# RWKV attention and an FFN in one launch: the bonus sums of chunk 1 by GpSimd and VectorE in place of TensorE, u's transfer in two parts, and a new order

## The chip, the cores and the metric

The kernel runs on one core of a Trainium2 chip. The core has TensorE (PE: matmuls; its weight loads are shown apart as PEld), VectorE (DVE), ScalarE (ACT), GpSimd (POOL) and SyncE (SP), which here only issues transfers; 16 DMA engines move data between HBM and the on-chip memory. TensorE writes to PSUM, which has eight banks of 512 float32 columns in 128 partitions. The metric is the time of one execution on the device in microseconds (us): 522.6, the median of three (520.49, 522.60, 523.03). The trace shown here is of a fourth execution, of 521.4 us.

## The reference

Inputs: r, k, v, w of shape 4 x 8 x 768 x 48 (batch, head, time, dimension), u of 8 x 48, and two FFN weights of 384 x 2048 and 2048 x 384, all float32. For each batch and head a 48 x 48 state runs through time; then each of the 3072 tokens goes through the FFN.

```
for t in range(S):
    cur = einsum('bhd,bhe->bhde', u * k[t], v[t])
    y[t] = einsum('bhd,bhde->bhe', r[t], state + cur)
    state = w[t][..., None] * state + einsum('bhd,bhe->bhde', k[t], v[t])
x = y.transpose(0, 2, 1, 3).reshape(B * S, H * D)
out = square(maximum(x @ w_in, 0)) @ w_out
```

The term of `cur` in y is, for each token and head, a scalar (the sum over d of r u k) times v. These scalars, 8 for each of 128 tokens of a unit, are the bonus sums.

## The kernel before

**The work.** Time is cut into 6 chunks of 128; a unit is one chunk of one batch, so there are 24. For a unit, running products of w (scans, L535) turn the recurrence into matmuls in the chunk and a state that is carried on. For chunks 0 and 1, TensorE turns w, k and r into the layout with the dimension on the partitions (`turn`, L516); for later chunks VectorE and transfers do it. Then `scores` (L750 for chunk 0, L671 for the rest), `mix` and the state's `outer` run on TensorE. A chunk's four units end in x, which is split into two float32r parts; the FFN goes over 16 blocks of 128 hidden units (f): 9 matmuls into one of two hp buffers (L860), relu and square on ScalarE and VectorE (L865 to L872), then 3 matmuls for each batch into the four ob banks (L878). Chunks 0 and 1 start their FFN in halves of two batches, so "hp at 0" to "hp at 11" are half blocks of 256 columns.

**The weights** come in eight groups (ri, ro for w_in and w_out as loaded; wi, wo as split). Each half of a group goes through ScalarE (L428), three VectorE steps on the bits (L432, L436, L441), ScalarE (L448) and a GpSimd subtraction (L449). All of it falls into the first 125 us.

**The bonus sums.** In chunks 0 and 1 (`c < 2`), VectorE multiplies the turned r and k into a buffer m (L550), TensorE multiplies that with u in 4 matmuls of 4 columns (`betas`, L575), for chunk 1 into an hp buffer, and ScalarE copies the result to beta in two copies (`place_betas`, L581). In chunks 2 to 5, GpSimd multiplies r by k and by -u as they were loaded, with time on the partitions (L584, L586), VectorE sums over the dimension (L589) and swaps halves between partitions in three small copies (`halves`, L592 to L594). From beta, ScalarE makes the diagonal blocks (L630, L745) on which `mix` builds.

**u** is loaded once, on ScalarE's queue, as one row repeated in all 128 partitions (un, L389); TensorE turns it for chunks 0 and 1 (L384), and GpSimd changes its sign for the later ones (L392).

**The order.** Each operation is a step of a plan with its engine, reads and writes; a table ORDER gives the order of all steps, found by a search beforehand, PLACES the buffer that each slot takes, and FILLS the places where a step on TensorE is preceded by filler: transposes of the identity into a free part of a bank (`fill`, L347), which nobody reads. An engine runs its steps strictly in that order. A step may not start before the steps whose data it reads or overwrites have ended. Some tiles lie on top of each other: chunk 1's x (`x1`) and the r, k, w of chunk 1's batches 2 and 3, and the raw weights of the last two groups and tiles of the first chunks.

Of the kernel before, what the change touches and what calls it, by code (L numbers as in the profile page):

```python
# [96 lines left out]
class Names:  # L97
# [132 lines left out]
def kernel(  # L230
# [11 lines left out]
    nc = tc.nc  # L242
# [34 lines left out]
    PC = J - D  # L277
# [48 lines left out]
    P = Plan()  # L326
# [129 lines left out]
    def attention(c, b, rank):  # L456
# [109 lines left out]

        rk = lambda: vals(1)
        beta = Slot("beta")
        if c < 2:
            bp = Slot("hp") if c else ps[0]  # L570
            bt = lambda: tl(bp) if c == 0 else bp.tile

# [446 lines left out]
```

## Time and profile before

| | |
|---|---|
| median of three executions | 522.6 us |
| the profiled execution | 521.4 us |
| its span in the trace | 519.7 us |
| TensorE busy | 506.6 us, 97% |
| VectorE busy | 358.3 us, 69% |
| ScalarE busy | 319.1 us, 61% |
| GpSimd busy | 87.8 us, 17% |
| HBM read, written | 31.65 MB, 4.72 MB |

The span is what the trace shows from the first to the last instruction; the execution's own time is 1.7 us longer. Busy times are the sum of an engine's instructions; matmuls are pipelined, so a busy TensorE need not be at its peak, and filler counts as busy. "idle before" names the wait of an engine and, behind an arrow, what ended it. The trace shows one matmul of float32 as two.

### The profile page before, as it was taken

How to read it: one execution, taken by the hardware profiler on the slowest of the kernel's cores; microseconds unless marked ns; L12 is line 12 of the kernel's file. 1: busy time of each engine (PE TensorE's matmuls, PEld its weight loads, DVE VectorE, ACT ScalarE, POOL GpSimd, SP SyncE). 2: the span in 40 equal slices, each digit the busy share in tenths (PEclk: the TensorE clock that was granted, in tenths of full speed). 3: DMA queues.
4: the chain of work that ended last, by engine and by line, in shares of the span. 5: the costliest groups of instructions: out<-in, count | busy, mean ns of one | idle time of the engine just before them, and what ended most of it. 6: DMA issues, size and time to landing. Idle time of an engine off the chain costs nothing.

```text
span 519.7 us, 13752 instructions
## 1 busy us (share of the span) xinstructions
PE 506.6 (97%) x5452; PEld 458.5 (88%) x5452; DVE 358.3 (69%) x787; ACT 319.1 (61%) x878; POOL 87.8 (17%) x133
## 2 busy tenths in 40 slices
PE   8999999999999999999998999999999999999996
PEld 7888898888999998899987989889988888998895
DVE  6999789898687988768778658678476354333332
ACT  4999898996766867666573656564543363433232
POOL 3025233344021040212203001303000000000000
PEclk9999999999999999999999999999999999999999
DMA  7999977363847765575772480661181000100001
GB/s 152 225 165 247 246 151 205 88 92 63 148 71 100 147 97 95 106 125 73 117 129 37 84 137 15 112 122 36 32 133 32 3 19 6 59 16 0 1 2 65
DMA packets 188310, 48.74 MB, mean 94 GB/s; under 512 B 178000, under 2 KB 183120, under 8 KB 188240
## 3 DMA queue, kind: packets, MB, share of 16 engines
q1 hardware_dynamic: 187520, 46.82, 47.6%
q8 instruction: 45, 0.74, 0.6%
q10 hardware_dynamic: 720, 0.98, 0.5%
q14 instruction: 25, 0.20, 0.1%
HBM read 31.65 MB, written 4.72 MB: 70 GB/s over the span
## 4 chain that ended last, share of the span: by engine, by line
PE 78%; SPq 5%; issue 5%; DVE 4%; ACT 4%; DMA 2%; POOL 1%; POOLq 0%; ACTq 0%; DVEq 0%
PE ob L878 35%; PE hp L860 34%; PE ob L668 2%; SPq L504 2%; PE ob L687 2%; DMA ri<-in_moe_w_in_dram 2%; PE a L677 2%; SPq L415 1%; PE a L650 1%; PE hp L635 1%; SPq L471 1%; POOL wi L449 1%; DVE pt L535 1%; ACT t L865 1%; DVE m L550 1%
## 5 line engine op out<-in xcount | busy, mean ns | idle before, releaser
L878 PE MATMUL ob<-wo,g 128*128 128x384 f32 x1152 | 227.0, 340 | 0.1
L860 PE MATMUL hp<-x,wi 128*128 128x512 f32 (+1 forms) x1062 | 221.8, 355 | 3.2 <-DVE g L872 2.5
L878 PEld LDWEIGHTS ob<-wo,g 128*128 128x128 f32 x1152 | 199.4, 188 | 8.1 <-DVE g L872 0.9
L860 PEld LDWEIGHTS hp<-x,wi 128*128 128x128 f32 x1062 | 174.1, 188 | 29.7 <-DVE g L872 3.7
L869 DVE SCALAR_TENSOR_TENSOR hp<-hp,t 128x512 f32<-128x512 f32 (+1 forms) x96 | 58.2, 606 | 74.5 <-ACT t L865 74.2
L865 ACT ACTIVATE t<-hp 128x512 f32<-128x512 f32 (+1 forms) x118 | 61.0, 517 | 72.2 <-PE hp L860 47.7
L872 DVE TENSOR_TENSOR g<-hp,g 128x512 fp32r<-128x512 f32 (+1 forms) x118 | 69.1, 587 | 35.5 <-ACT g L871 35.0
L871 ACT CAST g<-hp 128x512 fp32r<-128x512 f32 (+1 forms) x118 | 59.6, 506 | 49.5 <-DVE hp L869 48.6
L630 ACT ACTIVATE m<-diag,beta 128x64 f32<-128x64 f32 x160 | 40.4, 338 | 3.4 <-DVE beta L593 3.3
L658 POOL MEMSET S<- 1x1 f32 x20 | 2.2, 110 | 237.4 <-PE ob L668 237.4
L614 DVE SCALAR_TENSOR_TENSOR x<-ob,x 112x128 fp32r<-112x128 f32 x80 | 21.2, 284 | 19.3 <-ACT x L611 16.5
L822 ACT COPY ob<-zero 112x128 f32<-112x128 f32 x80 | 20.7, 270 | 17.3 <-PE ob L878 10.1
L611 ACT ACTIVATE x<-ob 112x128 fp32r<-112x128 f32 x80 | 19.1, 275 | 17.3 <-PE ob L687 12.1
L535 DVE TENSOR_TENSOR_SCAN pt<-pt,zero 112x128 f32<-112x128 f32 x64 | 27.2, 456 | 2.4 <-DMA x<-x 1.1
L449 POOL TENSOR_TENSOR wi<-q,wi 128x768 fp32r<-128x768 f32 x8 | 17.1, 2135 | 55.1 <-ACT wi L448 44.0
L584 POOL TENSOR_TENSOR st<-st 128x384 f32<-128x384 f32 x16 | 16.7, 1043 | 33.0 <-DVE st L480 32.5
L480 DVE STREAM_TRANSPOSE st<-st 128x1152 f32<-128x1152 f32 x16 | 21.6, 1363 | 0.0
L542 ACT ACTIVATE m<-pt 112x512 f32<-112x512 f32 x24 | 15.1, 631 | 9.2 <-DVE pt L535 8.2
L449 POOL TENSOR_TENSOR wo<-q,wo 128x768 fp32r<-128x768 f32 x8 | 15.9, 1983 | 18.1 <-ACT wo L448 14.8
L558 DVE TENSOR_TENSOR pt<-pt,m 112x512 f32<-112x512 f32 x24 | 16.9, 706 | 2.4 <-ACT Ec L557 1.3
L559 DVE SCALAR_TENSOR_TENSOR m<-pt,m 112x512 f32<-112x512 f32 x24 | 18.0, 748 | 0.3
L709 DVE COPY_PREDICATED m<-caus,a 128x256 f32<-128x256 uint8 x40 | 17.3, 439 | 0.9 <-PE a L650 0.9
(125 smaller groups left out, 540.0 us busy)
## 6 DMA issues: line engine op xcount, KB each, us to landing
pt<-st SPq DMA_DIRECT2D x96, 96.0 KB, 2.9
ro<-in_moe_w_out_dram SPq DMA_DIRECT2D x8, 768.0 KB, 6.1
v<-in_v_dram SPq DMA_DIRECT2D x96, 48.0 KB, 2.8
out_dram<-q SPq DMA_DIRECT2D x20, 192.0 KB, 2.1
ri<-in_moe_w_in_dram SPq DMA_DIRECT2D x32, 96.0 KB, 4.9
ri<-in_moe_w_in_dram SPq DMA_DIRECT2D x8, 384.0 KB, 6.1
st<-in_r_dram SPq DMA_DIRECT2D x8, 384.0 KB, 5.3
st<-in_w_dram SPq DMA_DIRECT2D x8, 384.0 KB, 4.9
```

The source lines that it names most:

```text
L449: P.add("pool", 1.9, rank(8 * k + 5), lambda q=q, tt=tt: G.tensor_tensor(out=tt[:, 1], in0=q.tile, in1=tt[:, 0].bitcast(F32), op=ALU.subtr ...
L480: V.transpose(out=zt[:, i].rearrange("a t p q i -> a t (p q) i"), in_=sv[:, :, i].rearrange("s t p q x -> s t (p q) x"))
L535: lambda p=p: V.tensor_tensor_scan(out=pt[:, 0, p], data0=src(0)[:, p], data1=zero.broadcast_to([HP, C]), initial=1.0, op0=ALU.mult, op1=A ...
L614: made.append(P.add("dve", c2, rank(nm + "l"), lambda y=y, hi=hi, lo=lo: V.scalar_tensor_tensor(out=lo(), in0=y(), scalar=-1.0, in1=hi().b ...
L630: A.activation(M.tile[:, o:o + Q], diag2, AF.Copy, scale=beta.tile[:, i:i + 1])
L822: P.add("act", 0.16, rank("zero"), lambda p=p: A.copy(out=obs[p][0:HP, DM:], in_=zero[0:HP].broadcast_to([HP, C])), w=[("YO", p)], after=t ...
L860: T.matmul(hp.tile[:, 0:n], wi[f][:, wl, kt], xT[:, kt, xl, xs], start=(m == 0), stop=(m == 3 * KT - 1))
L865: P.add("act", 0.49 if full else 0.28, rank("g1"), lambda: A.activation(t(), h(), AF.Relu), r=[hp], w=[(g, 1)])
L869: P.add("dve", 0.605 if full else 0.337, rank("g2"), lambda: V.scalar_tensor_tensor(out=h(), in0=h(), scalar=0.0, in1=t(), op0=ALU.max, op ...
L871: P.add("act", 0.48 if full else 0.26, rank("g3"), lambda: A.copy(out=hi(), in_=h()), r=[hp], w=[(g, 0)])
L872: P.add("dve", 0.605 if full else 0.335, rank("g4"), lambda: V.tensor_tensor(out=lo(), in0=h(), in1=hi().bitcast(F32), op=ALU.subtract), r ...
L878: T.matmul(obs[b][:, 0:DM], g.tile[0][:, gl, o:o + C], wo[f][:, wl], start=(f == 0 and m == 0), stop=(f == NF - 1 and m == 2))
```

## The change

1. In chunk 1 the bonus sums are made as in chunks 2 to 5: GpSimd multiplies twice, VectorE sums and swaps. The product on VectorE, the matmuls on TensorE and the copies on ScalarE stay for chunk 0 alone.
2. u's first transfer, on ScalarE's queue, fills one partition, and all of un is set to zero by VectorE beforehand (a wider memset). TensorE's turn of u, which takes the first row, stays. A second transfer of all 128 rows is issued on SP later, and GpSimd's change of sign comes behind it.
3. ORDER, PLACES and FILLS are new throughout. FILLS had 52 transposes at 12 places and has 57 at 13.

```
 ORDER = (
-    4, 14, 17, 19, 6, 16, 0, 5, 20, 1, 18, 26, 15, 11, 7, 23, 24, 25, 55, 58, 309, 21, 22, 27, 28, 8, 2, 13, 30, 9, 57, 31, 312, 59, 33, 56, 64, 10, 29, 61,
...
 FILLS = {
-    16: (2, 'ob', 1), 55: (6, 'ob', 3), 30: (3, 'ob', 1), 57: (4, 'ob', 1), 71: (2, 'ob', 0), 48: (5, 'ob', 1), 82: (3, 'ob', 3), 89: (5, 'ob', 1),
-    145: (3, 'ob', 0), 144: (7, 'ob', 0), 127: (8, 'side', 0), 168: (4, 'side', 0),
+    17: (3, 'ob', 1), 16: (3, 'ob', 2), 56: (3, 'ob', 1), 57: (4, 'ob', 1), 42: (3, 'ob', 1), 49: (2, 'ob', 1), 83: (3, 'ob', 3), 90: (18, 'ob', 1),
+    160: (4, 'ob', 0), 469: (2, 'ob', 0), 128: (2, 'side', 0), 130: (3, 'side', 0), 192: (7, 'side', 0),
 }
...
-    V.memset(front_un[:, 0:PC], 0.0)
+    V.memset(front_un, 0.0)
...
-        P.add("actq", 0.5, "un", lambda: nc.scalar.dma_start(out=un, in_=u.rearrange("h d -> (h d)").partition_broadcast(128)), w=["un"], runs=128, issue=0.36)
+        P.add("actq", 0.1, "u0", lambda: nc.scalar.dma_start(out=un[0:1], in_=u.rearrange("h d -> (h d)").partition_broadcast(1)), w=["un"], runs=1, issue=0.36)
         P.add("pe", 0.8, "ut", turn, r=["un"], w=[up])
         P.add("act", 0.25, "ut", spread, r=[up], w=["ut"])
+        P.add("sp", 0.5, "un", lambda: nc.sync.dma_start(out=un, in_=u.rearrange("h d -> (h d)").partition_broadcast(128)), w=["un"], runs=128, issue=0.6)
...
-        if c < 2:
+        summed = c == 0
+        if summed:
             P.add("dve", 0.62, rank("rk"), lambda: V.tensor_tensor(out=Ms[0].tile[0:HP].rearrange("a (g q t) -> a q g t", q=2, g=4), in0=turned(pt[:, 1]), in1=turned(src(2)), op=ALU.mult),
...
-        if c < 2:
+        if summed:
             bp = Slot("hp") if c else ps[0]
```

Three places of the order matter below. The first is TensorE behind the state matmuls of chunk 0's last batch, where the first of chunk 1's four groups with ut (L575) stands in the kernel before:

```order
L790 MATMUL a_153<-v_94,m_165 48x48
L860 MATMUL hp_152<-x_142,wi_57 128x256 x9
L575 MATMUL hp_151<-ut,m_167 128x4 x4
L878 MATMUL ob_147<-wo_67,g_97 128x384 x3
L878 MATMUL ob_148<-wo_67,g_99 128x384 x3
L860 MATMUL hp_151<-x_142,wi_57 128x256 x9
```

In the changed kernel, behind the same state matmuls (its lines are 2 higher):

```order
L792 MATMUL a_153<-v_94,m_166 48x48
L880 MATMUL ob_147<-wo_63,g_95 128x384 x3
L862 MATMUL hp_152<-x_142,wi_57 128x256 x9
L880 MATMUL ob_147<-wo_67,g_97 128x384 x3
L862 MATMUL hp_151<-x_142,wi_57 128x256 x9
L880 MATMUL ob_148<-wo_67,g_97 128x384 x3
```

No group with ut stands there or later, and the hp buffers pass from one block of the FFN to the next. The second place is GpSimd from the second half of weights 1 on (wo_63), before:

```order
L449 TENSOR_TENSOR wo_63<-q_155,wo_63 128x768
L449 TENSOR_TENSOR wo_67<-q_156,wo_67 128x768
L449 TENSOR_TENSOR wi_69<-q_155,wi_69 128x768
L449 TENSOR_TENSOR wo_75<-q_156,wo_75 128x768
L449 TENSOR_TENSOR wi_73<-q_155,wi_73 128x768
```

And in the changed kernel (wi_69 is the first half of weights 3):

```order
L450 TENSOR_TENSOR wo_63<-q_155,wo_63 128x768
L393 TENSOR_SCALAR un<-un 128x384
L450 TENSOR_TENSOR wo_67<-q_156,wo_67 128x768
L586 TENSOR_TENSOR st_143<-st_143 128x384
L588 TENSOR_TENSOR st_143<-st_143,un 128x384
L586 TENSOR_TENSOR st_143<-st_143 128x384
L588 TENSOR_TENSOR st_143<-st_143,un 128x384
L450 TENSOR_TENSOR wi_69<-q_155,wi_69 128x768
```

u's change of sign, which stood at the head of GpSimd's queue, and the products of chunk 1's batches 1 and 0 now stand between the subtractions; those of batches 2 and 3 stand in the same way before the second half of weights 6. The third place is VectorE's three steps on the first half of weights 0 (q_155 from ri_56), before:

```order
L432 TENSOR_SCALAR q_155<-q_155 128x768
L812 TENSOR_TENSOR S_137<-a_154,Ec_169 112x96
L436 SCALAR_TENSOR_TENSOR q_155<-ri_56,q_155 128x768
L441 SCALAR_TENSOR_TENSOR q_155<-ri_56,q_155 128x768
L550 TENSOR_TENSOR m_166<-pt_136,ob_149 112x2x4x64
L552 TENSOR_TENSOR pt_136<-pt_136 112x4x127
```

And in the changed kernel:

```order
L433 TENSOR_SCALAR q_155<-q_155 128x768
L814 TENSOR_TENSOR S_137<-a_153,Ec_169 112x96
L437 SCALAR_TENSOR_TENSOR q_155<-ri_56,q_155 128x768
L552 TENSOR_TENSOR m_166<-pt_136,ob_149 112x2x4x64
L554 TENSOR_TENSOR pt_136<-pt_136 112x4x127
L442 SCALAR_TENSOR_TENSOR q_155<-ri_56,q_155 128x768
```

Two products of chunk 0's batch 2 have moved ahead of the third step. SP's first transfers are the same in kind, in another order, and u's 128 rows are its 46th.

## Rows read from the trace of the kernel before

**Rows 1.** The page, part 1: busy us, share of the span, instructions.

```profile
PE 506.6 (97%) x5452; PEld 458.5 (88%) x5452; DVE 358.3 (69%) x787; ACT 319.1 (61%) x878; POOL 87.8 (17%) x133
```

**Rows 2.** Stretches: from:to, its us, busy us (instructions) of each engine, PEclk, DMA, GB/s.

```profile
5.30:28.00 22.70, 21.76 (x326) 19.20 (x327) 19.45 (x44) 17.79 (x56) 3.00 (x2) 1.00 0.93 202
...
28.00:58.00 30.00, 27.50 (x352) 24.66 (x351) 26.66 (x47) 27.33 (x72) 10.92 (x5) 1.00 0.95 218
...
58.00:112.00 54.00, 52.97 (x491) 47.76 (x490) 48.11 (x78) 50.62 (x119) 17.08 (x11) 1.00 0.74 160
...
120.00:510.00 390.00, 387.52 (x4103) 352.08 (x4094) 252.88 (x581) 212.36 (x603) 49.23 (x91) 1.00 0.41 70
```

**Rows 3.** Timeline of TensorE: start us, us, instruction, count. Two of four L575 groups.

```profile
58.74 0.95 PE L575 MATMUL hp<-ut,m 112*128 112x4 f32 x8
...
59.55 1.31 PE L878 MATMUL ob<-wo,g 128*128 128x384 f32 x6
...
107.80 1.05 PE L575 MATMUL hp<-ut,m 112*128 112x4 f32 x8
...
108.72 1.30 PE L878 MATMUL ob<-wo,g 128*128 128x384 f32 x6
```

**Rows 4.** Groups by line: shapes, count | busy us, mean ns | idle before.

```profile
L550 DVE TENSOR_TENSOR m<-pt 112x512 f32<-112x512 f32 x4 | 4.4, 1102 | 0.0
...
L584 POOL TENSOR_TENSOR st<-st 128x384 f32<-128x384 f32 x16 | 16.7, 1043 | 33.0 <-DVE st L480 32.5 <-issue 0.3 <-DVE hp L869 0.3
...
L586 POOL TENSOR_TENSOR st<-st,un 128x384 f32<-128x384 f32 x16 | 16.5, 1033 | 0.9
...
L589 DVE TENSOR_REDUCE beta<-st 128x8 f32<-128x384 f32 x16 | 8.7, 542 | 0.0
...
L581 ACT COPY beta<-hp 64x8 f32<-64x8 f32 x8 | 1.3, 157 | 0.1
...
L593 DVE TENSOR_TENSOR beta<-beta 64x4 f32<-64x4 f32 x16 | 2.8, 173 | 0.6
...
L351 PE MATMUL ob<-ident 128*128 128x128 f32 x52 | 8.1, 283 | 0.0
```

**Rows 5.** Timeline of GpSimd, two of its subtractions on weights.

```profile
49.75 2.36 POOL L449 TENSOR_TENSOR wo<-q,wo 128x768 fp32r<-128x768 f32 x1 [2.11 <-ACT wo L448]
...
64.00 2.22 POOL L449 TENSOR_TENSOR wi<-q,wi 128x768 fp32r<-128x768 f32 x1 [8.30 <-DMA ri<-in_moe_w_in_dram]
```

**Rows 6.** The page, parts 2 and 6: GB/s by slice; u's transfer.

```profile
GB/s 152 225 165 247 246 151 205 88 92 63 148 71 100 147 97 95 106 125 73 117 129 37 84 137 15 112 122 36 32 133 32 3 19 6 59 16 0 1 2 65
...
un<-in_u_dram ACTq DMA_DIRECT2D x1, 192.0 KB, 3.9
```

**Rows 7.** Timeline of TensorE, the head.

```profile
5.58 1.07 PE L518 MATMUL ob<-ident,st 128*112 128x128 f32 x4 [0.31 <-DMA st<-in_w_dram]
...
6.87 0.83 PE L518 MATMUL ob<-ident,st 128*112 128x128 f32 x4
```

**Rows 8.** Timelines of ScalarE and VectorE, the head.

```profile
8.20 0.68 ACT L545 ACTIVATE pt<-ob,one_sided 112x512 f32<-112x512 f32 x1
...
8.93 0.69 DVE L550 TENSOR_TENSOR m<-pt,ob 112x512 f32<-112x512 f32 x1 [0.87 <-ACT pt L545]
```

**Rows 9.** Timeline of TensorE, ahead of the first FFN matmul.

```profile
26.15 0.74 PE L351 MATMUL ob<-ident 128*128 128x128 f32 x5
...
26.83 0.68 PE L790 MATMUL a<-v,m 64*64 64x48 f32 x32
...
27.44 2.42 PE L860 MATMUL hp<-x,wi 128*128 128x256 f32 x18
```

**Rows 10.** Timelines of VectorE and TensorE near 52 us.

```profile
50.46 2.47 DVE L441 SCALAR_TENSOR_TENSOR q<-ro,q 128x768 uint32<-128x768 uint32 x1
...
53.31 0.65 PE L518 MATMUL hp<-ident,st 128*112 128x128 f32 x4 [0.87 <-DVE g L872]
```

**Rows 11.** One line of VectorE: count, ns min/median/max, first and last start.

```profile
L559 DVE SCALAR_TENSOR_TENSOR m<-pt,m x24: 676/684/1514, 11.3 to 425.6; 112x512 f32<-112x512 f32 x24
```

201 rows, old and new, of tables (ORDER, PLACES) are left out of this document.

## The prediction

> **What bounds the kernel now.** I read the busy times first: TensorE 97% of the span, VectorE 69%, ScalarE 61%, GpSimd 17% [rows 1]. Shares over the whole span mix stages, so next came the stretches. From 120 to 510 us TensorE is busy 387.5 of 390 us with the others far from full: there every matmul removed is time saved. The three stretches before, 5.3 to 112 us, hold the attention of chunks 0 and 1, the splitting of the weights, and all that this change touches; TensorE stands idle there for 106.70 - 102.23 = 4.5 us, and in the last of them (58 to 112 us) only 1.03 of 54 us, while ScalarE is idle for 3.4 and VectorE for 5.9 [rows 2]. So TensorE sets the pace, but with two neighbours close behind: that is the doubt in this case. The granted clock is 1.00 throughout, the level of 2.4 GHz, and no term hangs on it.
>
> **The change part by part.**
>
> *The products for the bonus sums leave TensorE.* Chunk 1 has four groups of L575, one for each batch: 4 matmuls, which the trace counts as 8. From the start of a group to the start of the next work: 0.81 us at 58.74, 0.92 at 107.80 [rows 3], and 0.81 for each of the two between. That is 3 x 0.81 + 0.92 = 3.35 us off TensorE, all within the stretch of 58 to 112 us where it is idle 2% of the time. ScalarE loses 8 copies of 0.157 = 1.26 us [rows 4]. Four tenancies of the two hp buffers, which the first FFN matmuls also use, go as well.
>
> *What comes in.* GpSimd gets eight products, four of 1.043 and four of 1.033 us: 8.3 us [rows 4]. They lie in two blocks of 4.15 us. The first comes, with the sign change of u, before the rest of weights 3; there GpSimd waits 8.30 us for a transfer today [rows 5], and the block with the sign change (1.17 us) takes 5.3: hidden. The second lies before the rest of w_out of group 6, whose first user (f = 12) comes several matmul groups later. VectorE loses four products (4.4 us as measured; 2.74 at 0.684, the median of L559 with the same shape) [rows 4, 11] and gets four sums of 0.542 and twelve swaps of 0.173: 4.2 us [rows 4]. So VectorE gains between -0.2 and +1.5 us. I take +1.4, because the long one among the four is a stall and not work. SP issues one transfer more, u's other rows; it stands as SP's 46th, behind chunk 1's r, and holds the queue behind it for one issue of 0.6 us; the loads of weights 3 and 4 wait behind it.
>
> *u's transfer.* Of 192 KB at the head one row stays. At the 152 GB/s of the first 13 us those 192 KB were 1.3 us of traffic, shared with w, r and k [rows 6]. TensorE's first transpose waits 0.31 us for w beyond its filler [rows 7], and that is all this end can give back. The next link is r's copy on ScalarE at 8.20, behind which VectorE starts at 8.93 after 0.87 us of idle time [rows 8]. It now stands ahead of the small copy of Ec, and r was turned at 7.70 [rows 7]: about 0.45 us. Together up to 0.76 us earlier. Against it stands the third shift step on weights 0: two products of batch 2, of 0.69 us each [rows 8], are now ahead of it, and the first FFN matmul hangs on that chain; today it starts at 27.44 [rows 9]. That may cost up to 1.4 us less what the head gained. I take -0.2 with the ends -0.8 and +1.0. The larger memset on VectorE lies ahead of its first scan, where it waits for TensorE, and u's single row has until r is turned.
>
> *Filler.* The table of fills has 57 in place of 52. Five cost 0.68 us at 26.15 [rows 9], so +0.7 us if nothing waits under them, 0 if it does. Eighteen of them now stand ahead of the outer products of batch 1: 2.4 us, just before the first FFN matmul. I take +0.7.
>
> *The order.* Every step of the first 120 us may stand elsewhere; from the last 250 steps of VectorE and ScalarE on nothing moved. The 4.5 us of idle time and the 52 x 0.136 = 7.1 us of filler [rows 2, 4] are what a new order can win; the 3.35 us are what it can fail to use. No row tells which; I take 0, with these ends.
>
> Sum: -3.35 + 0.7 - 0.2 = -2.85 us. The profiled execution took 521.4 us (span 519.7 and 1.7 around it), the three timed ones 522.6 in the middle, 520.49 to 523.03; the mean of all four is 521.9. So 521.9 - 2.85 = 519.0 us.
>
> **A rule that speaks against it.** A VectorE step on weights that started at 50.46 us took 2.47; a GpSimd subtraction ran from 49.75 to 52.11, so that the step ended 0.8 us after it, and TensorE then waited 0.87 us for the VectorE step behind [rows 5, 10]. The Trainium skill ("SBUF — State Buffer", Who interferes with whom) says that a VectorE instruction with two SBUF inputs and a GpSimd instruction that reads SBUF exclude each other for a whole instruction. By that rule the trace agrees here, and each new product can stop VectorE for its whole length, 8.3 us in all.
>
> **The rivals.**
>
> *ScalarE and VectorE take the place.* In 58 to 112 us a stretch shorter by 3.35 would be 50.65 us, with 49.6 us of TensorE, 50.62 - 1.26 = 49.4 of ScalarE and 48.11 + 1.4 = 49.5 of VectorE: all near 98%, which three engines that wait for each other have not reached in any stretch [rows 2]. If the most loaded stays where ScalarE is now (93.7%), the stretch gives back only 1.26/0.937 = 1.35 us; with the filler and the head that is -0.85: 521.0 us. For it: those rows. Against: the steps may slip past 112 us, where both have room.
>
> *The new order also closes old gaps.* Half of the 4.5 us of idle time beside the sum: 521.9 - 2.85 - 2.25 = 516.8 us. For it: several of the gaps are single waits for one VectorE step, as at 52.4 us [rows 10]. Against: more filler is laid in, not less.
>
> *GpSimd stops VectorE (slower).* Place: the two blocks. If all 8 products block in full, VectorE needs 49.5 + 8.3 = 57.8 us for the 54 us stretch: +3.8, with filler and head +4.3, 526.2 us. It eats into the gain from 50.65 - 49.5 = 1.1 us of blocking on, turns it into a loss from 54 - 0.5 - 49.5 = 4.0 us, and makes the kernel slower by over 0.5% from about 7.3 us on: nearly all eight. Against it: 32 such products run in chunks 2 to 5 today, and among 24 VectorE products of the same shape the longest of one line is 1.514 us against 0.684, so a hit there cost 0.8 us [rows 11].
>
> *The removed products were hidden.* Not likely: at 58.74 and 107.80 FFN matmuls follow at once [rows 3]. Then +0.5 and 522.4 us.
>
> **How the numbers follow.** My forecast 0.45 (its own range 517.4 to 520.0, by filler, head and 0.8 us of order); two neighbours full 0.26; gaps closed 0.14; hidden 0.08; VectorE stopped 0.07. 0.5% of 522.6 is 2.6 us, about what a measurement of this kernel can tell from no change: faster means under 520.0. The forecast gives 0.42 of its 0.45, the closed gaps 0.13, the full neighbours 0.03: 0.58. Slower, over 525.2, gets half of the last and a little for waits I have not seen: 0.06. The rest, 0.36, is within. The range, 515.8 to 522.4, leaves out the blocking case and the far ends of the order.
>
> **What would show it.** In the profile after: no matmul with ut as an input later than 40 us; TensorE's busy time down by 2.5 to 3.5 us; eight more GpSimd products near 1.04 us, the first four between 52 and 64 us with the rest of weights 3 not later than 67; VectorE products at 0.69 us with one or two over 1.2; the first copy on ScalarE before 8.0 us; the first FFN matmul between 26.5 and 28.5 us. TensorE's idle time in 58 to 112 us says which case it is: near 1 us for the forecast, over 2.5 us for the full neighbours. I am wrong if GpSimd waits for u's late rows, if VectorE has several steps over 2 us under the new products, or if chunk 1's first outputs on ScalarE wait for batch 3's sums, since they write over the tile that these read.

## The result, and the profile after

| | kernel before | changed kernel |
|---|---|---|
| median, us | 522.02 (520.49 to 523.03) | 527.77 (527.38 to 530.6) |
| profiled execution, its span, us | 521.4, 519.7 | 528.06, 526.3 |

The ratio is 1.0119 (95% interval 1.0091 to 1.0147): slower by 5.75 us where 519.0, 2.85 us less, was forecast. The time is outside the range.

The page of the changed kernel, part 1 (busy us, share, instructions), which answers to [rows 1]:

```profile
PE 506.8 (96%) x5425; PEld 457.3 (87%) x5425; DVE 368.8 (70%) x799; ACT 319.0 (61%) x870; POOL 98.6 (19%) x141
```

Its stretches, with the columns of [rows 2]:

```profile
5.30:28.00 22.70, 21.88 (x294) 19.20 (x292) 19.08 (x40) 17.59 (x55) 0.95 (x1) 0.92 0.95 203
28.00:58.00 30.00, 29.77 (x398) 26.66 (x397) 26.83 (x50) 27.87 (x72) 15.07 (x9) 1.00 0.88 200
58.00:112.00 54.00, 48.60 (x444) 41.52 (x444) 51.26 (x79) 46.59 (x106) 26.23 (x17) 1.00 0.80 167
112.00:125.00 13.00, 11.02 (x166) 9.32 (x166) 12.03 (x23) 6.80 (x18) 2.41 (x4) 0.87 0.10 17
```

VectorE is busy for 10.5 us more over the span, although at most 1.5 us more were forecast. In 58 to 112 us TensorE is idle for 5.4 us, against 1.03 before, and VectorE is busy 95%. That is the main place of the loss; from 112 to 125 us TensorE is idle another 2.0 us (not at all before), and from 28 to 58 us only 0.2, against 2.5 before. Where VectorE's time went is read from VectorE and GpSimd side by side. First GpSimd, from the rest of weights 2 on; the columns are start us, us, instruction:

```profile
56.37 1.02 POOL L586 TENSOR_TENSOR st<-st 128x384 f32<-128x384 f32 x1
57.47 1.21 POOL L588 TENSOR_TENSOR st<-st,un 128x384 f32<-128x384 f32 x1
58.65 1.72 POOL L586 TENSOR_TENSOR st<-st 128x384 f32<-128x384 f32 x1
60.45 1.20 POOL L588 TENSOR_TENSOR st<-st,un 128x384 f32<-128x384 f32 x1
63.41 1.83 POOL L450 TENSOR_TENSOR wi<-q,wi 128x768 fp32r<-128x768 f32 x1 [1.76 <-ACT wi L449]
...
108.25 2.30 POOL L450 TENSOR_TENSOR wo<-q,wo 128x768 fp32r<-128x768 f32 x1
115.74 1.82 POOL L450 TENSOR_TENSOR wi<-q,wi 128x768 fp32r<-128x768 f32 x1 [5.18 <-ACT wi L449]
```

VectorE in the same time:

```profile
56.44 1.36 DVE L433 TENSOR_SCALAR q<-q 128x768 uint32<-128x768 uint32 x1 [0.38 <-ACT q L429]
57.84 1.66 DVE L437 SCALAR_TENSOR_TENSOR q<-ri,q 128x768 uint32<-128x768 uint32 x1
59.42 1.36 DVE L433 TENSOR_SCALAR q<-q 128x768 uint32<-128x768 uint32 x1
60.71 0.41 DVE L874 TENSOR_TENSOR g<-hp,g 128x256 fp32r<-128x256 f32 x1
61.04 1.42 DVE L442 SCALAR_TENSOR_TENSOR q<-ri,q 128x768 uint32<-128x768 uint32 x1
...
63.59 0.53 DVE L591 TENSOR_REDUCE beta<-st 128x8 f32<-128x384 f32 x1
64.05 2.01 DVE L442 SCALAR_TENSOR_TENSOR q<-ro,q 128x768 uint32<-128x768 uint32 x1
...
100.54 1.64 DVE L437 SCALAR_TENSOR_TENSOR q<-ro,q 128x768 uint32<-128x768 uint32 x1
...
102.61 1.27 DVE L442 SCALAR_TENSOR_TENSOR q<-ro,q 128x768 uint32<-128x768 uint32 x1
103.80 1.51 DVE L554 TENSOR_TENSOR pt<-pt 112x508 f32<-112x508 f32 x1
105.41 1.32 DVE L560 TENSOR_TENSOR pt<-pt,m 112x512 f32<-112x512 f32 x1
...
108.78 2.32 DVE L554 TENSOR_TENSOR pt<-pt 112x508 f32<-112x508 f32 x1
111.02 0.68 DVE L874 TENSOR_TENSOR g<-hp,g 128x512 fp32r<-128x512 f32 x1
...
115.77 1.81 DVE L595 TENSOR_TENSOR beta<-beta 64x4 f32<-64x4 f32 x1
```

The two engines take turns. The shift step L433 takes 0.55 us when nothing is beside it and 1.36 beside a product; L437 0.95 and 1.66. Each ends some 0.4 to 0.8 us after the product that ran first, and the next product waits for it in turn: 1.72 and 1.20 us for 1.03. What has an input in PSUM (L874, 0.41) and the reduction (L591, 0.53) run at their own length. The second block of products, from 99.43 to 106.18 us, does the same to the four steps from 100.54 on: 1.64, 1.27, 1.51 and 1.32 us for 0.95, 0.95, 0.68 and 0.68. That makes eight stopped steps beside the eight products, 0.3 to 0.8 us each and 5.3 us in all. A weight subtraction does the same, and costs more since it is longer: 2.01 and 2.32 us for 0.95 and 0.69, and 1.81 us for a swap of four columns that takes 0.16.

TensorE, with what ended its idle time in brackets, has the other end of it:

```profile
61.17 0.44 PE L880 MATMUL ob<-wo,g 128*128 128x384 f32 x1 [0.71 <-DVE g L874]
66.76 1.34 PE L862 MATMUL hp<-x,wi 128*128 128x256 f32 x9 [0.81 <-DVE g L874]
87.02 2.37 PE L862 MATMUL hp<-x,wi 128*128 128x512 f32 x9 [1.38 <-DVE pt L536]
111.75 0.96 PE L880 MATMUL ob<-wo,g 128*128 128x384 f32 x4 [0.66 <-DVE g L874]
118.52 3.19 PE L880 MATMUL ob<-wo,g 128*128 128x384 f32 x9 [1.78 <-ACT ob L824]
```

The FFN's L874 is short and is not stopped, but it stands in VectorE's queue behind a step that is: at 111.02 behind the 2.32 us, and TensorE starts at 111.75. The wait at 118.52 names ScalarE; ScalarE in turn had waited for VectorE's chunk 1 outputs, which stood behind the swap of 1.81 us.

### The profile page after: what moved, and what is told of

Same layout as the page of the kernel before. It is cut to its first block, busy times and chain, and to the rows that moved or that the text cites. A ratio compares the mean times of both kernels' runs of the same rounds, so it can differ in the third digit from the quotient of the medians.

```text
span 526.3 us, 13737 instructions
## 1 busy us (share of the span) xinstructions
PE 506.8 (96%) x5425; PEld 457.3 (87%) x5425; DVE 368.8 (70%) x799; ACT 319.0 (61%) x870; POOL 98.6 (19%) x141
## 4 chain that ended last, share of the span: by engine, by line
PE 78%; DVE 9%; SPq 6%; DMA 3%; ACT 2%; issue 1%; POOL 0%; DVEq 0%; POOLq 0%
PE ob L880 34%; PE hp L862 33%; PE ob L670 2%; SPq L505 2%; PE ob L689 2%; SPq L416 2%; DMA ri<-in_moe_w_in_dram 2%; PE a L679 2%; DVE q L442 1%; PE a L652 1%; DMA ro<-in_moe_w_out_dram 1%; DVE g L874 1%; SPq L472 1%; PE hp L637 1%; DVE q L437 1%
## 5 line engine op out<-in xcount | busy, mean ns | idle before, releaser
L880 PE MATMUL ob<-wo,g 128*128 128x384 f32 x1152 | 229.5, 342 | 5.3 <-DVE g L874 2.9
L874 DVE TENSOR_TENSOR g<-hp,g 128x512 fp32r<-128x512 f32 (+1 forms) x118 | 68.9, 585 | 37.5 <-ACT g L873 37.0
L586 POOL TENSOR_TENSOR st<-st 128x384 f32<-128x384 f32 x20 | 22.6, 1134 | 32.8 <-DVE st L481 22.7
L588 POOL TENSOR_TENSOR st<-st,un 128x384 f32<-128x384 f32 x20 | 21.8, 1096 | 1.2
L554 DVE TENSOR_TENSOR pt<-pt 112x508 f32<-112x508 f32 x24 | 21.0, 877 | 0.6 <-ACT pt L522 0.4
```

The costliest lines, as they stand in the source:

```text
L586: P.add("pool", 0.97, rank("rk"), lambda: G.tensor_tensor(out=rk(), in0=rk(), in1=vals(2), op=ALU.mult), r=[(st, ui, 2)], w=[(st, ui, 1)])
L588: P.add("pool", 0.97, rank("ru"), lambda: G.tensor_tensor(out=rk(), in0=rk(), in1=un.rearrange("s (h d) -> s h d", d=D), op=ALU.mult), r=[ ...
L874: P.add("dve", 0.605 if full else 0.335, rank("g4"), lambda: V.tensor_tensor(out=lo(), in0=h(), in1=hi().bitcast(F32), op=ALU.subtract), r ...
L880: T.matmul(obs[b][:, 0:DM], g.tile[0][:, gl, o:o + C], wo[f][:, wl], start=(f == 0 and m == 0), stop=(f == NF - 1 and m == 2))
```

## The experiments

Theory 1: GpSimd's products and subtractions stop VectorE's instructions, and TensorE waits for what is queued behind those. Theory 2: the new order is the worse one, whatever the sums do. Theory 4: the products only hold up GpSimd's own queue, so that weights come late. (A third, that lower granted clocks make the difference, is taken up in the next section.) Each ratio is to runs of the kernel before on the same chip; "idle" is TensorE's idle time in 58 to 112 us, and VectorE's busy time is that of the profiled execution.

| run | median us | ratio, 95% | VectorE busy | idle |
|---|---|---|---|---|
| before | 522.0 | 1 | 358.3 | 1.03 |
| changed | 527.77 | 1.0119 (1.0091 to 1.0147) | 368.8 | 5.40 |
| e1_tiny | 523.11 | 1.0016 (0.9992 to 1.0040) | 361.5 | 4.19 |
| e2_memset | 522.61 | 1.0009 (0.9988 to 1.0029) | 360.7 | 3.23 |
| e3_sums | 534.72 | 1.0249 (1.0220 to 1.0278) | 363.1 | 8.76 |
| e4_head | 520.53 | 0.9978 (0.9960 to 0.9997) | 358.5 | 1.14 |
| e5_all_memset | 515.0 | 0.9868 (0.9817 to 0.9919) | 352.1 | 0 |
| e6_before_memset | 518.47 | 0.9933 (0.9905 to 0.9961) | 352.7 | 0 |
| e7_on_dve | 524.69 | 1.0053 (1.0022 to 1.0084) | 364.3 | 4.23 |
| e8_calm | 529.33 | 1.0141 (1.0094 to 1.0188) | 365.5 | 6.42 |
| e9_pieces | 524.11 | 1.0036 (1.0012 to 1.0061) | 357.5 | 4.95 |
| e10_head_pieces | 522.38 | 1.0005 (0.9983 to 1.0027) | 356.1 | 1.34 |
| e11_first_four | 524.39 | 1.0049 (1.0026 to 1.0072) | 364.0 | 4.98 |
| e12_second_four | 526.97 | 1.0100 (1.0064 to 1.0137) | 365.4 | 5.09 |

**The products cut short (e1_tiny).**

```
+        cut = (lambda x: x[:, 0:1, 0:4]) if c == 1 else (lambda x: x)
-  G.tensor_tensor(out=rk(), in0=rk(), in1=vals(2), op=ALU.mult)
+  G.tensor_tensor(out=cut(rk()), in0=cut(rk()), in1=cut(vals(2)), op=ALU.mult)      # and the same for un
```

> The changed kernel with chunk 1's eight GpSimd products cut to 4 elements a row (chunk 1's bonus sums are therefore left out of what is computed); VectorE's sums and swaps, the u transfers and the order stay. Theory 1 (GpSimd's products and subtractions stop VectorE instructions with two inputs in SBUF, VectorE is late, TensorE waits for it): the eight stops of 0.3 to 0.8 us go, about 5 us of VectorE's busy time, and the time falls from 527.8 to 521 to 524.5 us; what is left above 522 is the stops by the weight subtractions. Theory 2 (the new order is the worse one, whatever the sums do): 526 to 528 us. Theory 4 (the products hold up GpSimd's own queue, so that weights come late): falls too, to 521 to 524.5; the next run tells it from theory 1.

523.11 us: 4.7 us of the loss go with the eight products, in the same order. Theory 2 does not hold as the whole cause; that the time stays at 523 and not at 519 was left over.

**The products replaced by memsets (e2_memset).**

```
-  G.tensor_tensor(out=rk(), in0=rk(), in1=vals(2), op=ALU.mult)
+  for hs in (slice(0, H), slice(0, H), slice(0, H // 2)): G.memset(rk()[:, hs], 0.01)      # c == 1; the same for un
```

> The changed kernel with each of chunk 1's eight GpSimd products replaced by GpSimd memsets of the same place of about the same length (2.5 times 384 columns, about 1.05 us; chunk 1's bonus sums are left out of what is computed). GpSimd is as busy as in the changed kernel, but reads nothing from SBUF. Theory 1: VectorE is not stopped at those eight places and the time is that of the run with tiny products, 521 to 524.5 us. Theory 4 (GpSimd's queue): 526 to 528 us, as the changed kernel. Theory 2 (order): 526 to 528 us.

522.61 us, as with tiny products, although GpSimd is as busy. Its row of the timeline:

```profile
54.70 5.62 POOL L573 MEMSET st<- 128x384 f32 x12
```

VectorE's, there and at two later places:

```profile
55.57 0.96 DVE L437 SCALAR_TENSOR_TENSOR q<-ri,q 128x768 uint32<-128x768 uint32 x1
59.12 0.95 DVE L442 SCALAR_TENSOR_TENSOR q<-ri,q 128x768 uint32<-128x768 uint32 x1
...
71.78 2.26 DVE L442 SCALAR_TENSOR_TENSOR q<-ro,q 128x768 uint32<-128x768 uint32 x1
80.56 2.34 DVE L554 TENSOR_TENSOR pt<-pt 112x508 f32<-112x508 f32 x1
```

GpSimd works 5.62 us on end, and L437 takes 0.96 beside it, against 1.66 beside a product. So a GpSimd instruction that only writes does not stop these steps, which have two inputs in SBUF, and theory 4 falls. The Trainium skill ("SBUF — State Buffer", Who interferes with whom) says just that, of a VectorE instruction with two SBUF inputs; the rows agree. The last two rows show what is left over: steps of 2.3 us where subtractions run.

**The new sums in the old order (e3_sums, e8_calm).** The sums of the diff, in the order of before; the steps that went are replaced by the new ones near their places:

```
+  pool: rk, ru of batches 1, 0     behind the rest of w_out of weights 2
+  pool: rk, ru of batches 2, 3     e3: behind the rest of w_in of weights 6;  e8: behind the memsets of chunk 1's first mix
+  dve:  beta, bh of each batch     near the places of the removed rk and bp steps
```

> The kernel before, its order and its u transfer, with the new sums alone: chunk 1's products on GpSimd behind the second half of weights 2 (batches 1, 0) and behind the first half of weights 6 (batches 2, 3), the sums and swaps on VectorE where TensorE's and ScalarE's steps stood. Theory 1: TensorE's busy time falls by 3 us or more, but VectorE is stopped and the gain is eaten: 521 to 526 us, with over 4 us more of VectorE in 28 to 112 us. Theory 2 (the order alone is at fault): the forecast's own sum holds, 518 to 521 us.

534.72 us, far outside what either theory said. TensorE's row shows a wait of my own making:

```profile
107.66 1.14 PE L691 MATMUL ob<-m,v 64*64 64x64 f32 x32 [5.24 <-POOL v L663]
```

GpSimd's rows ahead of it:

```profile
99.82 1.82 POOL L452 TENSOR_TENSOR wi<-q,wi 128x768 fp32r<-128x768 f32 x1 [5.42 <-ACT wi L451]
101.60 1.35 POOL L588 TENSOR_TENSOR st<-st 128x384 f32<-128x384 f32 x1
103.02 1.59 POOL L590 TENSOR_TENSOR st<-st,un 128x384 f32<-128x384 f32 x1
104.58 1.70 POOL L588 TENSOR_TENSOR st<-st 128x384 f32<-128x384 f32 x1
106.36 1.19 POOL L590 TENSOR_TENSOR st<-st,un 128x384 f32<-128x384 f32 x1
107.49 0.09 POOL L662 MEMSET S<- 1x1 f32 x1
107.52 0.09 POOL L663 MEMSET v<- 1x1 f32 x1
```

Two memsets of 0.09 us, which stand in the middle of a TensorE step, had come to lie behind four products. The run says nothing on theory 2, so it was made again with the products behind these memsets, and with u's change:

> The kernel before in its order, with u's change and the new sums, the products of batches 2 and 3 now behind the two small memsets that chunk 1's first TensorE step waits for (the earlier run had them ahead of these, and TensorE waited 5.2 us there). Base is the run with u's change alone, 520.5 us. Forecast's sum: 518 to 519.5 us. Theory 1: the products stop VectorE here too, and 2 to 6 us of TensorE's idle time come back with them: 520 to 525 us. If the new order is what hurts: 518 to 519.5 us as well.

529.33 us: 8.8 us over the same order with u's change and the old sums (e4_head). TensorE's waits of that kernel in 26 to 130 us name VectorE alone for more than 0.4 us (line waited for: us, times, longest):

```profile
PE hp L865 <- DVE g L877: 5.5, 5, 2.0
PE ob L883 <- DVE g L877: 2.4, 1, 2.4
PE hp L522 <- DVE g L877: 0.8, 1, 0.8
```

So the old order is no better a place for these sums: put into it by hand, they take it to 1.6 us above the changed kernel, which is within the noise of the two. Part of the 8.8 us can be the placing by hand, as in e3. The 520 to 525 us that I gave theory 1 were too low all the same.

**u's transfer alone (e4_head).** The lines of the diff on un, and the SP transfer behind the second load of weights 3, in the order of before.

> The kernel before, its order and its sums, with the change of u's transfers alone: one row first, all rows later on the SP queue with the negation on GpSimd behind the second half of weights 1. Forecast's term: -0.2 us (-0.8 to +1.0), so 521.2 to 523 us beside 522.0; GpSimd's negation of 1.9 us may stop one VectorE instruction. If the head were the fault: 524 us or more.

520.53 us, less than before by 1.1 us by the ratio and 1.7 by the medians on the same chip; under the 521.2 expected. Its first turn starts at 5.07 us (5.58 before), VectorE's first product at 8.43 (8.93) and the first FFN matmul at 26.91 (27.44): 0.5 us that stay. It is the only run with all of the computation that beats both kernels.

**The subtractions replaced by memsets (e5_all_memset, e6_before_memset).** In the changed kernel of e2, and in the kernel before:

```
-  G.tensor_tensor(out=tt[:, 1], in0=q.tile, in1=tt[:, 0].bitcast(F32), op=ALU.subtract)
+  for n in (2 * DM, 2 * DM, DM): G.memset(tt[:, 1, 0:n].bitcast(F32), 0.0)
```

> The changed kernel with chunk 1's eight products and also the sixteen weight subtractions on GpSimd replaced by GpSimd memsets of about the same length (chunk 1's bonus sums and the low parts of the weights are left out of what is computed). Nothing on GpSimd reads SBUF in 28 to 112 us any more. Theory 1, in its wide form (the run without products stayed at 522.6 us because the weights' subtractions still stop VectorE, now at places where TensorE waits for it): TensorE's idle time in 58 to 112 us falls from 3.2 us to about 1, and the time comes to 518.5 to 520.5 us, the forecast. Rival (the new order leaves its own waits, for PSUM banks and for chunk 1's late first step): 521.5 to 523 us, idle over 2.5 us.

> The kernel before with its sixteen weight subtractions on GpSimd replaced by memsets of about the same length (the low parts of the weights are left out of what is computed). Theory 1: its few stops (seven of 0.3 to 1.7 us, about 7 us of VectorE) lie mostly beside TensorE's work, so little comes back: 520.3 to 521.8 us. If GpSimd's reads cost the kernel before as much as the changed one: 518 to 520 us.

One thing in the first expectation is not so: u's change of sign on GpSimd, at 50.51 us in e5, and a small product (S by Ec) of 0.50 us at 109.91 still read SBUF in 28 to 112 us.

515.0 and 518.47 us: both fall further than expected, and their difference, 3.5 us, is the forecast's sum (2.85) within the intervals. Page and stretch of the first:

```profile
PE 501.3 (98%) x5425; PEld 454.7 (89%) x5425; DVE 352.1 (69%) x799; ACT 317.8 (62%) x870; POOL 95.7 (19%) x189
...
58.00:112.00 54.00, 54.00 (x597) 48.26 (x596) 48.59 (x97) 50.96 (x118) 24.60 (x48) 1.00 0.78 165
```

and of the second:

```profile
PE 504.1 (98%) x5452; PEld 457.4 (89%) x5452; DVE 352.7 (68%) x787; ACT 318.9 (62%) x878; POOL 86.5 (17%) x165
...
58.00:112.00 54.00, 54.00 (x497) 49.69 (x496) 47.24 (x85) 52.23 (x128) 20.02 (x31) 1.00 0.74 159
```

TensorE is not idle for a moment of 58 to 112 us in either, in the new order too; the rival reading, that the new order has its own waits there, falls. TensorE's busy time differs by 2.8 us, where -3.35 + 0.7 = -2.65 was worked out. The reads that were replaced cost the kernel before 3.2 us and the changed one 12.8: 5.2 by the products (changed to e2) and 7.6 by the very same sixteen subtractions (e2 to e5; without them but with the products the kernel was not run). VectorE's busy time says it too: it goes from 368.8 to 360.7 to 352.1 us, 16.7 us less, against 5.6 less in the kernel before. That the subtractions themselves came late is not the way: TensorE's waits that name GpSimd are 0.4 us in the kernel before, 0.3 in the changed one and 0.4 in e2, from 5 to 128 us.

The memsets are not quite free of stops. Five times in e6 and three times in e5 the shift, which has one input in SBUF, took 0.77 to 1.21 us for 0.55 beside one. One of them, GpSimd and VectorE in e6:

```profile
59.59 2.32 POOL L429 MEMSET wi<- 128x768 f32 x3 [6.60 <-DVE g L876]
...
59.71 1.03 DVE L436 TENSOR_SCALAR q<-q 128x768 uint32<-128x768 uint32 x1 [0.24 <-ACT q L432]
```

So these two runs show a little less than the whole price of the stops.

**The products on VectorE (e7_on_dve).**

```
-  P.add("pool", 0.97, rank("rk"), lambda: G.tensor_tensor(...)
+  P.add("dve" if c == 1 else "pool", 0.97, rank("rk"), lambda: (V if c == 1 else G).tensor_tensor(...)      # ru likewise
```

> The changed kernel with chunk 1's eight products on VectorE in place of GpSimd, at the same places of the order. Theory 1: GpSimd's eight products already cost VectorE about 5.3 us in stops; eight products of 0.69 us on VectorE itself are 5.5 us, so nothing is lost: 525 to 528.5 us beside 527.8. Rival (GpSimd takes the work off VectorE, the stops being small): 530 us or more.

524.69 us, 3 us better than with GpSimd and better than I had said: eight products done by VectorE itself cost it less than eight on GpSimd.

**GpSimd's work in pieces (e9_pieces, e10_head_pieces).**

```
+  for x in range(0, 2 * DM, DM // 2): G.tensor_tensor(out=tt[:, 1, x:x + DM // 2], ...)      # e9: products in four too
```

> The changed kernel, everything computed, with the GpSimd work cut into pieces: each weight subtraction in four of 192 columns, each of chunk 1's products in four of 96. Theory 1, with a stop that lasts to the end of the GpSimd instruction that is under way: the longest stop falls from 1.4 us (subtraction) and 0.8 us (product) to about 0.5 and 0.3, VectorE's busy time falls by some 5 us, and the time comes to 521 to 524.5 us. Rival (pieces come one right after the other and VectorE does not get between them, or it stands for each): 527 us or more. If all the loss went, 519 us.

> The kernel before with u's change (520.5 us alone) and each weight subtraction on GpSimd in four pieces of 192 columns; everything is computed. Theory 1: the kernel before lost 3.2 us to GpSimd's subtractions (518.5 us with memsets in their place); pieces give back up to two thirds of it: 518 to 520 us. Rival (pieces do not help): 520 to 522 us.

524.11 us for the changed kernel, as expected; but 522.38 for the kernel before with u's change, by the medians 1.9 us worse than whole (1.4 by the ratios, whose intervals overlap). One subtraction of that kernel in GpSimd's timeline, and one of its two groups by line (count | busy us, mean ns | idle before):

```profile
74.88 3.70 POOL L434 TENSOR_TENSOR wi<-q,wi 128x192 fp32r<-128x192 f32 x4 [5.80 <-ACT wi L457]
...
L434 POOL TENSOR_TENSOR wo<-q,wo 128x192 fp32r<-128x192 f32 x32 | 24.7, 803 | 11.3 <-ACT wo L457 7.9 <-issue 3.5
```

A quarter takes 0.80 us on average, a whole one took 1.98: now GpSimd stands, between its pieces, for VectorE. TensorE then waited 1.1 and 0.8 us for the late weights. Pieces do not do away with the exclusion; they give the turn to VectorE.

**Which products (e11_first_four, e12_second_four).** The cut of e1 for `c == 1 and b in (2, 3)`, and for `(0, 1)`.

> The changed kernel with only the second four products (batches 2 and 3) cut to 4 elements a row; the first four (batches 1 and 0, in GpSimd's long wait before the rest of weights 3) stay whole. (The sums of batches 2 and 3 are left out of what is computed.) The prediction had the first four hidden in that wait: then 522.5 to 523.5 us, as with all eight cut. Theory 1: the first four stop VectorE for about 2.8 of the 5.3 us: 525 to 526.5 us.

> The changed kernel with only the first four products (batches 1 and 0) cut to 4 elements a row; the second four stay whole. (The sums of batches 0 and 1 are left out of what is computed.) If the first four were hidden and the second carry the loss: 527 to 528 us. Theory 1, with the stops of the second four at 2.5 of the 5.3 us: 524.5 to 526.5 us.

524.39 and 526.97 us, where all eight cut gave 523.11: by the medians the first four cost 1.3 us, the second four 3.9. VectorE's busy time rises by 2.5 and 3.9 us over that of e1. That the second four cost more is just beyond the noise (1.0100 beside 1.0049); that about half of the first block's stops are hidden and nothing of the second's is only what the medians suggest. Neither expectation fits closely.

## Why the prediction was wrong

*The step that failed* is "GpSimd gets eight products ... hidden", and with it the chance of 0.07 for "GpSimd stops VectorE". The products were priced by GpSimd's own idle time [rows 5] and not by VectorE's. The rival had the mechanism and its place, and its price for full blocking, 526.2 us, was near the outcome. It was argued away by [rows 11]: 32 such products run in chunks 2 to 5, and the longest of 24 steps took 0.8 us too long. That row was misread. Its longest step stood beside a weight subtraction, not beside a product (kernel before, GpSimd and VectorE):

```profile
123.03 1.84 POOL L449 TENSOR_TENSOR wo<-q,wo 128x768 fp32r<-128x768 f32 x1 [0.41 <-ACT wo L448]
...
123.91 1.51 DVE L559 SCALAR_TENSOR_TENSOR m<-pt,m 112x512 f32<-112x512 f32 x1
```

And one line could not show the products' hits: beside the 32 products of that trace, seven VectorE steps of other lines (L535, L552, L558, L592) took 0.2 to 0.9 us too long. Those chunks lie where VectorE is busy 253 of 390 us, 65%; in 58 to 112 us it is 89% [rows 2], and there the eight products stopped eight steps. What was wrong is how often a product hits, and what hangs on it.

*The price of the rival was also too small in kind.* It counted the eight products, which cost 5.2 us. The sixteen subtractions that both kernels have cost 3.2 us in the kernel before and 7.6 in the changed one: 4.4 us more, by the intervals some 3 us either way, where the sum had "Order" at 0. That 526.2 came near the measured time without this part is luck. Why the subtractions cost more there is not shown. Without the replaced reads VectorE is busy 48.6 us of 58 to 112 us in the changed kernel (e5) and 47.2 in the kernel before (e6), which is little; what stands behind a stopped step is set by the order. The threshold as worked out, a loss from 4.0 us of blocking on, was not tested by itself.

*The forecast's own terms, without those reads.* TensorE: -2.65 worked out, -2.8 measured (e5 against e6). VectorE's net was to be 1.4 us more ("-0.2 to +1.5"); its busy time is 0.6 us less in e5 than in e6, outside that range. The shifts stopped by memsets, 2.0 us in e6 and 0.9 in e5, account for some of it: without them it is an estimated 0.5 more. The head: -0.2 with -0.8 to +1.0 given; 0.5 us in the trace of e4_head and 1.1 by its ratio (0.2 to 2.1), so near the lower end or under it. In the profiled execution of the changed kernel that gain was lost again: ScalarE's first copy starts at 6.92 us (before 8.0 was expected), but the first FFN matmul at 29.35, outside the 26.5 to 28.5, behind 18 fills and a stretch of low clock. It is not the fills: in e2, with the same order and fills and a clock of 1.00 from 15 to 20 us, it starts at 27.37. Order, at 0: with the subtractions' stops alone the new one leaves TensorE idle for 3.23 us of 58 to 112 us (e2) where the old one leaves 1.03, and without them both leave none.

*"ScalarE and VectorE take the place"* (521.0) named the fuller neighbour rightly, but without the exclusion VectorE at 90% did not cost TensorE anything (e5). *"The new order closes old gaps"*: only there, with 0 us idle. *"The removed products were hidden"* falls by e5 and e6.

*Of the signs listed*: no ut matmul after 35.5 us; the rest of weights 3 at 63.41; GpSimd did not wait for u's late rows (its sign change began at 52.00, behind a subtraction); chunk 1's first outputs on ScalarE waited for TensorE, not for batch 3's sums. The sign "VectorE has several steps over 2 us under the new products" did not come: the five steps over 2 us in 58 to 112 us all stand beside subtractions, and the longest beside a product took 1.66. TensorE's idle time in 58 to 112 us, "over 2.5 us" for full neighbours, is 5.4. TensorE's busy time was to fall by 2.5 to 3.5 and rose by 0.2 in this execution, for the reason that follows; in e2, which has the same matmuls and a clock of 1.00 in both of the stretches below, it is 503.4, a fall of 3.2.

*Not settled*: what a lower granted clock adds. In the profiled execution the clock was 1.00 before and in these two stretches of the changed kernel well under it, between its two levels of 1.2 and 2.4 GHz (columns of [rows 2]):

```profile
15.00:20.00 5.00, 4.99 (x53) 4.14 (x49) 3.60 (x8) 3.58 (x16) 0.00 (x0) 0.66 0.82 165
118.00:122.00 4.00, 3.48 (x22) 3.04 (x26) 3.97 (x8) 3.22 (x8) 0.00 (x0) 0.58 0.00 0
```

The second follows TensorE's wait of 1.78 us. TensorE's busy time stands 506.8 - (506.6 - 2.65) = 2.85 us above the forecast's, an estimate of what it took in this execution. Yet an execution at a mean clock of 0.998 took 527.49 us, so it is not the cause of the median, and an execution of e9_pieces at 0.945 took 525.06, only 1 us over that kernel's median. How much it adds to each run was not measured by itself.

## What to carry to other kernels

Before work goes to GpSimd, look at VectorE's load in the stretch where it will run, not at GpSimd's idle time: beside a VectorE that was busy nine tenths of the time, eight products stopped eight steps, where 32 in a stretch at 65% stopped seven, and what counts is what TensorE waits for behind such a step. A rate of hits read in a calmer stretch must not be carried over, and a long step is evidence only once it is known what ran beside it. To price such contention, replace the suspected instruction by one of the same length that only writes: the time that it gives back is the cost of the exclusion with queue and order kept, less what the writes themselves still stop (here the one-input shift).

## What was not expected of the hardware

- Two operands are not needed to be stopped: the shift L433, with one SBUF input, took 1.36 us for 0.55 beside a product. The reduction L591 never took over 0.55 us. The Trainium skill ("SBUF — State Buffer", Who interferes with whom) has both, the first as a two-port mode of tensor_scalar. Nor does that shift need a read on GpSimd: beside memsets it took up to 1.21 us (e6).
- A stop does not depend on the size of the stopped step: a swap of 64x4 took 1.81 us for 0.16.
- Kernels in which TensorE waited more also ran at a lower mean clock; what drives what was not tested: 0.997 for the runs of before, 0.996 without GpSimd's reads (e5), 0.990 and 0.988 in e8 and e3.
